# Column groups for the block-diagonal products, a sign check on one partition, ten in-place weight buffers and a new order

## The chip, the cores and the metric

The kernel runs on one core of a Trainium2 chip. The core has five engines with an instruction queue each: TensorE (PE, matmuls into PSUM), VectorE (DVE), ScalarE (ACT), GpSimd (POOL, which works on SBUF only here) and SyncE (SP, which here only issues loads). The outputs are issued from ACT's queue. The metric is the time of one launch on the device in microseconds (us). Before the change it is 217.35 us, the median of three runs (216.36 to 217.43).

## The reference

`x` is 4 x 11456 x 128, `inducing` is 32 x 128. Per batch, 32 inducing rows attend to all tokens (`h`), and then all tokens attend to these 32 rows. Each token of that result goes to one of 8 experts by the largest cosine with the expert's embedding, and through that expert's two matrices, weighted by its gate:

```python
h = mab(I, x)                 # softmax(I x' / sqrt(C)) x : 32 x 128
x = mab(x, h)                 # softmax(x h' / sqrt(C)) h : 11456 x 128
xn = x / (norm(x) + 1e-6);  en = emb / (norm(emb) + 1e-6)
logits = xn @ en.T / tau
e = argmax(logits)            # gate = softmax(logits)[e]
out = gate * (relu(x @ w1[e]) @ w2[e])     # F = 1024 hidden units
```

Since a token's row is a weighted sum of the 32 rows of `h`, norms, logits and hidden units can all be had from its 32 weights. The kernel uses one expert per batch, found from the mean of `h`. If for each hidden unit either all 32 rows keep the same sign, or the sum is sure to have it, the two layers and the ReLU fold into one 32 x 128 matrix `L` per batch. A check proves that this holds; a list of items (batch, expert) that need more is worked off in a loop behind the main program, which is empty for this data.

## The kernel before, in words

A batch's tokens are six blocks: five of 2048 tokens and one of 1280 (320 columns per group of partitions, the others 512). A block lives as 128 partitions (4 groups of 32 weights) x 512 columns.

- **Stage 1** (`stage1`, `own`, `finish`): scores of the block against the inducing rows (L476), their maxima (L536, DVE), the exponentials (L551, ACT), transposes (L574), sums over tokens (L597). Batch 0 transposes three of its own x blocks (L504) instead of loading them. `finish` joins the four groups into `hT` (L677, DVE) by small matmuls (L621, L635, L655, L671, L672), makes the tables `HB` and `gbd` (L737, L738), and picks the expert (L690 to L697), whose weights SP then loads (L728, L729).
- **Stage 2** (`stage2`), per block: scores against `hT` (L767), maxima (L773), their spreading (L778), differences (L784), weights `e` (L789, ACT), the product with the block-diagonal `HB` (L795), its copy `hq` (L801, ACT), `hq * e` (L805, POOL), squared norms (L809), the products with `gbd` (L817, L818) and their transposition (L825). When the blocks of a gate have come through, `gate` works out the gate's values for them: roots, reciprocals, logits (L888), maxima, exponentials, signs, the choice, and at the end `v` (L927, L942) and the gate values `f` (L946).
- **Stage 3** (`stage3`), per block: `fb` spreads the gate values (L1111, DVE), POOL multiplies (L1115, `pf`), PE multiplies with `L` in four row groups (L1134), ACT copies four pieces of PSUM to `o` (L1141) and issues the output's transfer.
- **`fold`** makes `L` out of the expert's weights (L969 to L1031), with the sums that the check needs (L996 to L1007). **`check`** runs its comparison on all 128 partitions (L1043 to L1083) and then `left` (L1091 to L1100) marks what is left to do.

Batch b's stages 2 and 3 run beside stage 1 of batch b+1; the last batch's stages 2 and 3 have nothing beside them. Python code (`Plan`) sets the order: each piece of work has an engine, an estimated duration, dependencies, buffers it takes and frees and a priority from tables of numbers (`FIRST`, `LATE`, `START`, `HOLD`, `NEAR`). The instructions are then emitted in the planned order, and each engine executes its own in that order. `fill` puts matmuls on zeros (L1228, `wz`) where the plan sees PE idle. Buffers are rings: `BUFS` has their lengths (xT 7, x 3, e 7 and so on), and PSUM has 8 banks.

Of the kernel before, what the change touches and what calls it, by code (L numbers as in the profile page):

```python
# [60 lines left out]
FIRST = dict(G=-28.5, L=-60, at=-5, both=6.5, chk=12, chose=43.5, chosen=-23.5, copy_s=-59, count=36, den=53, diff=-31, em=-31, eq=-29.5,  # L61
             evict=58.5, ex=56, expA=33, expB=-25.5, expert=20, f=12.5, fin=-56.5, first=-27, fix=-28, flags=-59.5, fours=-4, fw=-47,
             gat=-8, get_ax=-11, get_w=60, get_x=-1.5, get_xT=-40, gm=10, gm4=7.5, gmb=60, good=16, gv=44, hT=3, hTc=-29, hb=-11.5,
             hj=4.5, hs=-19.5, inv=19, keep_e=-7, keep_hq=-59, keep_x=59.5, left=-31.5, lg=29.5, li=-56, lm=-4, mat=60, mk=-60,
             mults=-10, nb=-6.5, newton=4.5, norm=44, outs=44.5, parts=-24.5, pick=13.5, pick_vals=-1, places=60, prod=9.5, put_h=-60,
             put_li=59.5, put_o=5, r1=6, rm=-17, root=3.5, root_e=60, rows=-22, score=-56, scores=1, se=-12.5, seen=60, selr=55.5,
             sides=4.5, sides2=30.5, signs=44, some=-32, spread=-35, spread_f=-20.5, square=-7.5, square_e=-52, squared=-0.5, sums=15.5,
             times=32.5, top=60, top_e=9.5, turn=26.5, turn_e=-20, turn_s=22, under=54, vals=-29, vp=60, vpb=-30.5, weigh=-26.5,
             zf=-16.5, zs=-5, zz=-15)
# [1319 lines left out]
```

## Time and profile before

| | before |
|---|---|
| time, median of 3 runs | 217.35 us (216.36 to 217.43) |
| the profiled execution | 215.55 us, span 213.9 us |
| mean granted TensorE clock | 0.982 |
| busy: PE / DVE / ACT / POOL | 188.5 / 156.4 / 130.5 / 116.9 us |
| moved by DMA | 72.24 MB, 338 GB/s over the span |
| `hT` of the batches ready (L677 starts) | 31.1, 70.1, 112.6, 153.6 us |

The span is the time from the first to the last instruction; the rest of the execution's time lies around it. The busy times are sums over the whole program, and the program has three parts with different loads: up to 31 us stage 1 of batch 0 and the loads, from there to 154 us three stretches in which stages 2 and 3 of one batch and stage 1 of the next run together, and from there to the end the last batch alone. So the views by stretch say more than the sums.

### The profile page before, as it was taken

Reading aid. Unit: us, or ns where it says so; the run is one execution under the profiler, and the core shown is the slowest. Engines: PE = TensorE matmul, PEld = TensorE weight load, DVE = VectorE, ACT = ScalarE, POOL = GpSimd, SP = SyncE. Lnnn points to the kernel's source line nnn. Section 1 sums busy time; section 2 is a strip of 40 time slices with the busy share of each in tenths; the row PEclk is TensorE's granted clock in tenths of the full one; section 3 lists DMA queues with packets and bytes.
Section 4 is the critical chain, followed back from the end, with each engine's and each line's share of the span. In section 5 each row is a group of like instructions: output and inputs, shape, how many; then the busy total and the mean of one; then the engine's idle time right before and its main releaser. Section 6 shows DMA issues by size and latency. Waiting matters only on the chain.

```text
span 213.9 us, 5217 instructions
## 1 busy us (share of the span) xinstructions
PE 188.5 (88%) x1894; PEld 96.4 (45%) x1894; DVE 156.4 (73%) x433; ACT 130.5 (61%) x302; POOL 116.9 (55%) x232
## 2 busy tenths in 40 slices
PE   7999999999999978799999998899999997796740
PEld 2566652445465434354754344467524433332120
DVE  6544738998995789799688989986589988835230
ACT  2286612462765824267977556779688886876820
POOL 2100000267677734067677674859468989898710
PEclk9999999999999999999999999999999999999975
DMA  6999999999979999998789999994779854349781
GB/s 207 428 424 414 372 415 417 366 424 412 420 254 322 407 348 429 421 415 367 267 279 343 418 428 421 421 406 159 291 201 426 365 202 196 149 165 395 296 367 51
DMA packets 12222, 72.24 MB, mean 338 GB/s; under 512 B 1624, under 2 KB 2144, under 8 KB 4896
## 3 DMA queue, kind: packets, MB, share of 16 engines
q1 hardware_dynamic: 7984, 48.12, 58.0%
q10 hardware_dynamic: 4208, 23.75, 27.1%
q8 instruction: 16, 0.26, 0.5%
q14 instruction: 14, 0.11, 0.1%
HBM read 48.13 MB, written 23.72 MB: 336 GB/s over the span
## 4 chain that ended last, share of the span: by engine, by line
PE 33%; POOL 26%; DVE 17%; DMA 12%; issue 6%; ACT 3%; SPq 0%; DVEq 0%; POOLq 0%
POOL pf L1115 7%; DMA xT<-in_xT 6%; DMA w1t<-in_w 5%; PE ps L476 5%; PE ps L597 5%; POOL hq L805 4%; PE ps L1134 3%; PE ps L574 3%; PE ps L504 3%; PE ps L1228 2%; PE ps L795 2%; DVE mxb L778 2%; PE ps L767 2%; DVE mx L773 2%; DVE d L784 2%
## 5 line engine op out<-in xcount | busy, mean ns | idle before, releaser
L805 POOL TENSOR_TENSOR hq<-hq,e 128x512 f32<-128x512 f32 (+1 forms) x24 | 29.0, 1208 | 48.2 <-ACT hq L801 48.1
L1141 ACT COPY o<-ps 128x512 f32<-128x512 f32 (+1 forms) x94 | 47.5, 569 | 9.5 <-PE ps L1134 7.5
L1115 POOL TENSOR_TENSOR pf<-e,fb 128x512 f32<-128x512 f32 (+1 forms) x24 | 28.9, 1206 | 7.2 <-PE ps L1134 4.8
L1134 PE MATMUL ps<-pf,L 32*128 32x512 f32 (+1 forms) x192 | 26.4, 612 | 1.2 <-POOL pf L1115 0.9
L795 PE MATMUL ps<-e,HB 128*128 128x512 f32 (+1 forms) x48 | 25.0, 606 | 1.1 <-ACT e L789 0.6
L801 ACT COPY hq<-ps 128x512 f32<-128x512 f32 (+1 forms) x24 | 13.4, 557 | 17.5 <-PE ps L795 16.5
L476 PE MATMUL ps<-xT,indT_sb 128*32 128x512 f32 x160 | 21.0, 602 | 3.1 <-DMA xT<-in_xT 2.6
L789 ACT ACTIVATE e<-d 128x512 f32<-128x512 f32 (+1 forms) x24 | 14.5, 604 | 12.7 <-DVE R L784 12.0
L597 PE MATMUL ps<-x,pt 128*32 128x128 f32 x608 | 20.8, 275 | 0.7 <-issue 0.5
L767 PE MATMUL ps<-xT,hT 128*32 128x512 f32 x160 | 19.7, 600 | 1.4 <-ACT L L1031 0.6
L551 ACT ACTIVATE s<-ps,nb 128x1024 f32<-128x1024 f32 (+3 forms) x15 | 13.5, 899 | 11.8 <-DVE nb L543 6.6
L597 PEld LDWEIGHTS ps<-x,pt 128*32 128x32 f32 x608 | 16.0, 109 | 8.5 <-issue 3.8
L1111 DVE STREAM_TRANSPOSE fb<-f 128x512 f32<-128x512 f32 (+1 forms) x24 | 15.3, 661 | 4.3 <-POOL f L946 3.0
L536 DVE TENSOR_REDUCE mk<-ps 128x1 f32<-128x1024 f32 (+3 forms) x15 | 14.1, 941 | 4.2 <-PE ps L476 2.6
L809 DVE TRANSPOSE_TENSOR_REDUCE nn<-hq 128x16 f32<-128x512 f32 (+1 forms) x24 | 15.8, 658 | 1.5 <-POOL hq L805 1.3
L778 DVE STREAM_TRANSPOSE mxb<-mx 128x512 f32<-128x512 f32 (+1 forms) x24 | 16.3, 678 | 0.8
L784 DVE CUSTOM_DVE_ANT_0 d<-mxb,ps 128x512 f32<-128x512 f32 (+1 forms) x24 | 15.5, 648 | 1.3
L773 DVE TRANSPOSE_TENSOR_REDUCE mx<-ps 128x16 f32<-128x512 f32 (+1 forms) x24 | 15.8, 658 | 0.5 <-PE ps L767 0.5
L1228 PE MATMUL ps<-wz 128*128 128x512 f16 x59 | 15.7, 398 | 0.0
L817 PE MATMUL ps<-e,gbd 128*128 128x256 f32 (+1 forms) x48 | 14.9, 392 | 0.8 <-ACT o L1141 0.8
L818 PE MATMUL ps<-e,gbd 128*128 128x256 f32 (+1 forms) x48 | 13.6, 366 | 0.0
L817 PEld LDWEIGHTS ps<-e,gbd 128*128 128x128 f32 x48 | 8.0, 189 | 11.5 <-issue 5.1
(190 smaller groups left out, 329.1 us busy)
## 6 DMA issues: line engine op xcount, KB each, us to landing
xT<-in_xT SPq DMA_DIRECT2D x20, 1024.0 KB, 11.4
out<-o ACTq DMA_DIRECT2D x20, 1024.0 KB, 4.4
x<-in_xP SPq DMA_DIRECT2D x17, 1024.0 KB, 10.8
xL<-in_xT SPq DMA_DIRECT2D x4, 640.0 KB, 14.9
out<-o ACTq DMA_DIRECT2D x4, 608.0 KB, 7.9
x<-in_xP SPq DMA_DIRECT2D x4, 512.0 KB, 3.9
w1t<-in_w SPq DMA_DIRECT2D x4, 512.0 KB, 10.0
w2t<-in_w SPq DMA_DIRECT2D x4, 512.0 KB, 12.2
```

The source lines that it names most:

```text
L476: nc.tensor.matmul(ps[32 * j:32 * j + 32, :].rearrange("p (g i) -> p g i", i=128), lhsT=indT_sb, rhs=v[:, j], start=True, stop=True)
L597: nc.tensor.matmul(ph.t[32 * j:32 * j + 32, 0:C], lhsT=pt.t[:tw, tat[k] + g, 32 * j:32 * j + 32], rhs=x, start=k == ks[0] and g == 0, stop ...
L767: nc.tensor.matmul(ps[32 * j:32 * j + 32, :W].rearrange("p (t i) -> p t i", i=32), lhsT=st.hT[:, 0:M], rhs=v[:, j], start=True, stop=True)
L773: nc.vector.tensor_reduce(new(mx)[:, :T], b1.t[:, :W].rearrange("p (t i) -> p t i", i=32), AX.X, ALU.max, apply_transpose=True)
L778: nc.vector.transpose(new(mxb)[:, :W], mx.t[:, :T].unsqueeze(2).broadcast_to([P, T, 32]))
L795: nc.tensor.matmul(new(b2)[:, :W], lhsT=st.HB, rhs=e.t[:, :W], start=True, stop=True)
L805: nc.gpsimd.tensor_tensor(paired(hq.t[:, :W]), paired(hq.t[:, :W]), halved(e.t[:, :W]), ALU.mult)
L817: nc.tensor.matmul(b3.t[:, :H], lhsT=st.gbd[:, 16:], rhs=e.t[:, :H], start=True, stop=False)
L1115: nc.gpsimd.tensor_tensor(new(pf)[:, :W], st.e[k].t[:, :W], fb.t[:, :W], ALU.mult)
L1134: nc.tensor.matmul(new(pcs[j])[:, :W], lhsT=st.L[32 * j:32 * j + 32, :], rhs=pf.t[32 * j:32 * j + 32, :W], start=True, stop=True)
L1141: (nc.vector.tensor_copy if dve else nc.scalar.copy)(v[:, j], pcs[j].t[:, :W].rearrange("c (t i) -> c t i", i=32))
L1228: nc.tensor.matmul(ps_all[:, b], lhsT=wz[:, 0:P], rhs=wz, start=True, stop=True)
```

## The change

1. **Column groups.** A helper `quads` splits a stationary matrix of 128 columns into four of 32 columns, each a matmul of its own into 32 partitions of PSUM. It is used for `HB`, both `gbd` products, the tables, and the small products of `finish`, `fold` and `check`. The transposes of 128 x 128 stay whole. Row transposes of one column become plain matmuls with the identity. The scores (L476, L767) and L597 have been in such column groups all along.
2. **Sign check on one partition.** `fold` now works out the ratio `less / more` and its maximum over all partitions in the shadow of other work (`over`, `share`, `worst`, `worst_t`, `worst1`); `check` compares one number with it. Three POOL operations of the check (`good`) go. `left` shrinks from eight or nine POOL operations to three, one of which, `chose`, waits only for `seen`; `vp` makes a table `rest` beforehand.
3. **Weights in one buffer.** `mxb`, `d`, `e` and `pf` of a block become one buffer `e` that is overwritten in place, from a ring of 10; the x ring grows from 3 to 4 and f from 3 to 5. In the last batch odd blocks put their output through a buffer of the x ring.
4. **Moves between engines.** The scaling of `sel` goes from DVE to ACT, the addition in `both` (L911) from POOL to ACT (`se9`), one step of `sides2` from POOL to ACT (`both_sides`).
5. **Gates.** The last batch has two gates of three blocks instead of three gates of 3, 2 and 1.
6. **Order.** All priority tables, and the planner's durations; it now counts a switch of the array's mode.

```diff
-GATES = [[(0, 1, 2), (3, 4, 5)]] * 3 + [[(0, 1, 2), (3, 4), (5,)]]
+GATES = [[(0, 1, 2), (3, 4, 5)]] * 4
-BUFS = dict(xT=7, xL=2, x=3, xR=1, s1=2, pt=1, mxb=2, d=2, e=7, hq=2, gts=2, lg=2, ex=1, fb=2, pf=2, o=3, mx=2, nn=2, f=3)
+BUFS = dict(xT=7, xL=2, x=4, xR=1, s1=2, pt=1, e=10, hq=2, gts=2, lg=2, ex=1, fb=2, o=3, mx=2, nn=2, f=5)
-FIRST = dict(G=-28.5, L=-60, at=-5, both=6.5, chk=12, chose=43.5, chosen=-23.5, copy_s=-59, count=36, den=53, diff=-31, em=-31, eq=-29.5,
+FIRST = dict(G=-12, L=-60, at=-39.5, bad1=7, both=-25.5, both_sides=-59.5, chk=12.5, chose=-55.5, chosen=60, copy_s=-49, den=-50.5,
...
-        t = max(clock[o.eng], o.after)
+        t = max(clock[o.eng] + (self.SWITCH if o.eng == PE and o.mode != self.mode else 0.0), o.after)
...
+    def quads(out, lhsT, rhs, start=True, stop=True):
+        for q in range(0, lhsT.shape[-1], M):
+            nc.tensor.matmul(out[q:q + M], lhsT=lhsT[:, q:q + M], rhs=rhs, start=start, stop=stop)
...
+        def sel():
             t["selr"] = small.tile([P, 1], F32, name="selr")
-            nc.vector.tensor_tensor(t["selr"], rz, t["fw"], ALU.mult)
+            nc.scalar.activation(t["selr"], t["rz"], AF.Identity, scale=t["fw"])
             t["sel"] = small.tile([P, P], F32, name="sel")
-            nc.vector.tensor_scalar(t["sel"], flat(sel4), t["selr"], None, ALU.mult)
-        c(DVE, 0.9, selr, free=[b3])
+            nc.scalar.activation(t["sel"], flat(sel4), AF.Identity, scale=t["selr"])
+        c(ACT, 0.5, sel)
...
-            nc.vector.transpose(new(mxb)[:, :W], mx.t[:, :T].unsqueeze(2).broadcast_to([P, T, 32]))
+            nc.vector.transpose(new(e)[:, :W], mx.t[:, :T].unsqueeze(2).broadcast_to([P, T, 32]))
...
-            nc.scalar.activation(new(e)[:, :W], d.t[:, :W], AF.Exp, scale=-SCALE)
+            nc.scalar.activation(e.t[:, :W], e.t[:, :W], AF.Exp, scale=-SCALE)
...
-            nc.tensor.matmul(new(b2)[:, :W], lhsT=st.HB, rhs=e.t[:, :W], start=True, stop=True)
+            quads(new(b2)[:, :W], st.HB, e.t[:, :W])
...
-            nc.tensor.matmul(b3.t[:, :H], lhsT=st.gbd[:, 16:], rhs=e.t[:, :H], start=True, stop=False)
-            nc.tensor.matmul(b3.t[:, :H], lhsT=st.gbd[:, :P], rhs=e.t[:, H:W], start=False, stop=True)
+            quads(b3.t[:, :H], st.gbd[:, 16:], e.t[:, :H], stop=False)
+            quads(b3.t[:, :H], st.gbd[:, :P], e.t[:, H:W], start=False)
...
+        def se9():
+            nc.scalar.activation(t["se"], t["se"], AF.Identity, bias=nano)
         def both():
-            nc.gpsimd.tensor_scalar(t["se"], t["se"], 1.0, 1e-9, ALU.mult, ALU.add)
             nc.gpsimd.tensor_tensor(t["se"], t["se"], t["zz"], ALU.mult)
...
-            nc.gpsimd.tensor_scalar(up, t["pos"], 2.0, -1.0, ALU.mult, ALU.add)
-            nc.gpsimd.tensor_tensor(up, up, t["ss"], ALU.mult)
+        def both_sides():
+            nc.scalar.activation(t["up"], t["ss"], AF.Abs, bias=tiny)
+        def over():
+            nc.vector.reciprocal(t["more"], t["more"])
+        def share():
+            nc.gpsimd.tensor_tensor(t["less"], t["less"], t["more"], ALU.mult)
+        def worst():
+            nc.vector.tensor_reduce(t["wo"], t["less"], AX.X, ALU.max)
+        def worst_t():
+            nc.tensor.matmul(new(pw)[0:1, 0:P], lhsT=t["wo"], rhs=ident, start=True, stop=True)
+        def worst1():
+            nc.vector.tensor_reduce(st.worst, pw.t[0:1, 0:P], AX.X, ALU.max)
+            nc.vector.tensor_scalar_add(st.worst, st.worst, SURE)
...
-        def good():
-            nc.gpsimd.tensor_scalar(t["em"], t["em"], ROOM, None, ALU.mult)
-            nc.gpsimd.tensor_scalar(ok, st.more, t["em"], None, ALU.mult)
-            nc.gpsimd.tensor_tensor(ok, ok, st.less, ALU.subtract)
+        def bad1():
+            nc.vector.tensor_scalar(pad1[0:1, 1:2], t["em"], st.worst, None, ALU.is_lt)
...
+        def chose():
             nc.gpsimd.tensor_scalar(sn, sn, 0.0, None, ALU.max)
+        def left():
+            nc.gpsimd.tensor_scalar(st.rest, st.rest, wipe[:, st.b, 0:1], None, ALU.max)
+            nc.gpsimd.tensor_tensor(present[:, 0:n, st.b], st.seen[:, 0:n], st.rest.unsqueeze(1).broadcast_to([P, n, E]), ALU.mult)
...
-            nc.gpsimd.tensor_tensor(new(pf)[:, :W], st.e[k].t[:, :W], fb.t[:, :W], ALU.mult)
+            nc.gpsimd.tensor_tensor(e.t[:, :W], e.t[:, :W], fb.t[:, :W], ALU.mult)
...
-        o = plan.buf("o")
+        o = plan.buf("x" if st.b == NB - 1 and k % 2 else "o")
```

The new order shows at three places. The first is POOL's queue at the program's end, the last batch's. Before, the third gate (10 columns), the check's bookkeeping on `vq`, `present` and `seen`, and then the last block's product:

```order
L942 TENSOR_SCALAR v<-v,vp 128x10
L946 TENSOR_TENSOR f<-v,se 128x10
L1091 TENSOR_SCALAR vq<-wipe 128x1
L1092 TENSOR_TENSOR vq<-vq,vp 128x1
L1093 TENSOR_SCALAR present<-rev,vq 128x8
L1094 TENSOR_SCALAR present<-present 128x8
L1096 TENSOR_SCALAR seen<-seen 128x24
L1098 TENSOR_TENSOR seen<-seen 128x8 x2
L1099 TENSOR_TENSOR present<-present,seen 128x8
L1100 TENSOR_TENSOR present<-present,wipe 128x1
L1115 TENSOR_TENSOR pf<-e,fb 128x320
```

And now, where L1157 is the product (in place, on `e`) and L978 and L982 are `v` and `f` of the second and last gate:

```order
L978 TENSOR_SCALAR v<-v,vp 128x42
L1136 TENSOR_SCALAR seen<-seen 128x16
L982 TENSOR_TENSOR f<-v,se 128x42
L1141 TENSOR_SCALAR rest<-rest,wipe 128x8
L1142 TENSOR_TENSOR present<-seen,rest 128x2x8
L1157 TENSOR_TENSOR e<-e,fb 128x512 x2
L1157 TENSOR_TENSOR e<-e,fb 128x320
```

The bookkeeping shrank from nine instructions to three, and two more blocks' products now stand behind the last gate.

The second place is DVE's queue around the last batch's `hT`, with the batch before it in its gates. Before:

```order
L660 TENSOR_SCALAR rz<-ps 128x1
L661 RECIPROCAL rz<-rz 128x1
L663 TENSOR_TENSOR selr<-rz,fw 128x1
L665 TENSOR_SCALAR sel<-sel_133,selr 128x128
L825 STREAM_TRANSPOSE gts<-ps 128x160
L809 TENSOR_REDUCE nn<-hq 128x10
L609 SCALAR_TENSOR_TENSOR hj<-hj,fix,ps 128x128
L677 COPY hT<-ps 128x128
```

And now, where L708 is the copy into `hT`, L926, L940, L963 and L974 are the gates' `lm`, `se`, `v` and reciprocal, and L1153 is `fb`:

```order
L963 TENSOR_REDUCE v<-lg 128x48
L969 TENSOR_REDUCE seen<-lg 128x8
L926 TENSOR_REDUCE lm<-lg 128x42
L974 RECIPROCAL se<-se 128x48
L637 SCALAR_TENSOR_TENSOR hj<-hj,fix,ps 128x128
L687 TENSOR_SCALAR rz<-ps 128x1
L688 RECIPROCAL rz<-rz 128x1
L1153 STREAM_TRANSPOSE fb<-f 128x512 x2
L940 TENSOR_REDUCE se<-ex 128x42
L708 COPY hT<-ps 128x128
```

Work of both gates of the batch before, which followed `hT`, now stands ahead of it.

The third is PE's queue behind the last batch's `hT`. Before, with L795, L817 and L818 as whole matmuls between scores in column groups (L767) and outputs in row groups (L1134):

```order
L767 MATMUL ps<-xT,hT 32x512 x8
L1134 MATMUL ps<-pf,L 128x512 x4
L795 MATMUL ps<-e,HB 128x512
L817 MATMUL ps<-e,gbd_143 128x256
L818 MATMUL ps<-e,gbd_143 128x256
L1056 MATMUL ps<-r_2315,ones 128x1
L767 MATMUL ps<-xT,hT 32x512 x4
```

And now, where L372 is `quads`, L800 the scores and L1176 the outputs:

```order
L800 MATMUL ps<-xT,hT 32x512 x12
L1176 MATMUL ps<-e,L 128x512 x4
L372 MATMUL ps<-e,HB 32x512 x4
L800 MATMUL ps<-xT,hT 32x512 x4
L372 MATMUL ps<-e,gbd_137 32x256 x8
```

Scores and block-diagonal products now have the same shape of tile, and PE goes from one to the other without a change of it.

More of the change, by code (lines that the diff above doesn't have):

```diff
@@ L1 @@
+import math
 from contextlib import ExitStack
@@ L59 @@
 SLOT = 6
-FIRST = dict(G=-28.5, L=-60, at=-5, both=6.5, chk=12, chose=43.5, chosen=-23.5, copy_s=-59, count=36, den=53, diff=-31, em=-31, eq=-29.5,
[L62 to L69, printed above, removed]
@@ new lines @@
+LATE = dict(G=-47.5, L=43, at=-20.5, bad1=-39, both=6.5, both_sides=-7, chk=-25.5, chose=43, chosen=-13, copy_s=19.5, den=-17,
+            diff=-59.5, em=-21, eq=-60, evict=-46, ex=-12, expA=30, expB=-3.5, expert=-36, f=6, fin=41, first=-15.5, fix=7.5, flags=5.5,
+            fours=-20, fw=23, gat=-39, get_ax=-16, get_w=54, get_x=-23, get_xT=-49, gm=-9, gm4=58.5, gmb=-10.5, gv=60, hT=-60, hTc=25.5,
+            hb=-46.5, hj=25, hs=6, inv=-45, keep_e=32.5, keep_hq=-36, keep_x=18.5, left=-25, lg=-35.5, li=55, lm=-60, mat=30.5, mk=-60,
+            mults=39.5, nb=23, newton=-15.5, norm=-0.5, outs=44, over=-6, parts=56, pick=53, pick_vals=58, places=58.5, prod=-48,
+            put_h=39.5, put_li=24, put_o=22, r1=58, rm=59.5, root=-60, root_e=23, rows=60, score=-60, scores=-10.5, se=-52, se9=-30,
+            seen=25.5, sel=-51.5, selr=-60, share=-12, sides=-20, sides2=-1.5, signs=26, some=10, spread=26.5, spread_f=-48, square=40.5,
+            square_e=-42, squared=-30, sums=-6.5, times=-60, top=11.5, top_e=-2.5, turn=47, turn_e=60, turn_s=39, under=-30, vals=49.5,
+            vp=32, vpb=-52, weigh=41.5, worst=-28, worst1=5, worst_t=-29, zf=-59, zs=51.5, zz=-10)
@@ L654, in fin @@
         def fin():
-            nc.tensor.matmul(new(b3)[:, 0:1], lhsT=flat(sel4), rhs=t["z"], start=True, stop=True)
-        c(PE, 0.24, fin, take=[b3])
+            quads(new(b3)[:, 0:1], flat(sel4), t["z"])
+        c(PE, 0.22, fin, take=[b3])
         def selr():
@@ L712, in vpb @@
         def vpb():
[L713 to L714 removed]
+            quads(new(b6)[:, 0:1], ones, pad1[:, 0:1])
+        c(PE, 0.22, vpb, take=[b6])
         def vp():
@@ new lines, in sides2 @@
+        def sides2():
+            t["more"] = small.tile([P, NCH], F32, name="more")
+            t["less"] = small.tile([P, NCH], F32, name="less")
+            nc.gpsimd.tensor_tensor(t["more"], t["sa"], t["up"], ALU.add)
+            nc.gpsimd.tensor_tensor(t["less"], t["sa"], t["up"], ALU.subtract)
+        o_2 = plan.add(POOL, 0.46, sides2, deps=[o_sa, o_up], when=when)
+        def over():
+            nc.vector.reciprocal(t["more"], t["more"])
+        o_2 = plan.add(DVE, 0.13, over, deps=[o_2], when=when)
```

288 lines of the change are left out of this document (145 added, 143 removed).

## The prediction

> **What bounds the kernel now.** I read the page's sums and chain first, then the busy times by stretch, then the chain in order of time, and last the single queues where the chain runs through them.
>
> ```profile
> span 213.9 us, 5217 instructions
> PE 188.5 (88%) x1894; PEld 96.4 (45%) x1894; DVE 156.4 (73%) x433; ACT 130.5 (61%) x302; POOL 116.9 (55%) x232
> GB/s 207 428 424 414 372 415 417 366 424 412 420 254 322 407 348 429 421 415 367 267 279 343 418 428 421 421 406 159 291 201 426 365 202 196 149 165 395 296 367 51
> PE 33%; POOL 26%; DVE 17%; DMA 12%; issue 6%; ACT 3%; SPq 0%; DVEq 0%; POOLq 0%
> ```
>
> By the sums POOL, busy for 55%, would be the last engine to look at. But the chain gives it 26% of the span, second to PE only. The stretches are cut where the batches' `hT` are ready, where the last batch's first gate ends, and where the last output is issued:
>
> ```profile
> core 0: us, PE busy (x) PEld busy (x) DVE busy (x) ACT busy (x) POOL busy (x), PEclk, DMA share, GB/s
> 31.10:72.00 40.90, 39.34 (x431) 20.38 (x433) 34.45 (x88) 22.23 (x51) 22.41 (x39) 1.00 0.97 377
> 72.00:112.50 40.50, 36.61 (x414) 19.68 (x407) 34.64 (x82) 24.02 (x55) 22.07 (x46) 1.00 0.94 363
> 112.50:153.60 41.10, 39.08 (x428) 20.57 (x427) 33.60 (x85) 29.60 (x66) 26.98 (x45) 1.00 0.89 360
> 153.60:184.70 31.10, 27.80 (x184) 12.13 (x184) 27.40 (x70) 24.33 (x57) 26.64 (x52) 1.00 0.68 259
> 184.70:207.10 22.40, 16.29 (x98) 6.05 (x96) 10.39 (x34) 15.01 (x37) 16.94 (x43) 0.98 0.75 309
> ```
>
> In the three middle stretches PE is busy for 115.0 of 122.5 us; DVE has 34 us of 41 and POOL 22 to 27. Behind 153.6 PE, DVE and POOL are close together, and behind 184.7 no engine is dense by its busy time, but the chain shows what the order does there:
>
> ```profile
> 160.22 1.28 POOL pf L1115
> ...
> 161.58 0.24 POOL se L911
> ...
> 161.90 0.27 POOL se L912
> ...
> 174.32 0.26 POOL n L874
> ...
> 177.47 0.81 POOL lg L888
> ...
> 181.64 0.24 POOL se L911
> ...
> 184.68 0.29 POOL f L946
> ...
> 187.71 0.58 POOL lg L888
> ...
> 192.66 0.18 POOL n L874
> ...
> 194.10 0.42 POOL v L942
> ...
> 194.84 0.28 POOL lg L888
> ...
> 195.19 0.24 POOL em L1066
> ...
> 196.15 1.22 POOL pf L1115
> 197.38 0.28 POOL lg L897
> 197.66 1.22 POOL pf L1115
> ...
> 200.81 0.17 POOL vq L1091
> ...
> 203.31 0.83 POOL pf L1115
> ```
>
> From 160.2 to 204.1 the chain is POOL's own queue with a few short steps of DVE between: an operation that goes from POOL there shortens the run, until the next engine binds.
>
> **The end: POOL's part.** Differences of starts in that fence give the prices, gaps of issue included. The bookkeeping `left` takes 203.31 - 200.81 = 2.5 us; its three successors are small operations like L911 and L912, 0.3 us each by 161.90 - 161.58, so 0.9 in all: 1.6 us less, once for each of the last two batches. The check's three operations take 196.15 - 195.19 = 0.96 us, also twice. The addition L911 goes three times, 0.32 each: 1.0. The third gate costs 194.10 - 192.66 = 1.44 for its root, 0.35 and 0.28 for its logits (from 194.84 to 195.19, and L897), and 200.81 - 198.88 = 1.93 from the end of the last big product to the bookkeeping: 4.0 us. Against that the second gate grows by 80 columns of logits; L888 took 0.81 us for 384 and 0.58 for 256, so 0.15 for each of three passes, 0.5 us. In sum 3.2 + 1.9 + 1.0 + 4.0 - 0.5 = 9.6 us of POOL's queue. Not all of it can come off:
>
> - *153.6 to 184.7.* Here 3.2 us of it lie (one `left`, one check, two additions). But DVE is busy for 27.4 of the 31.1 us, and its work there stays: the same maxima, spreadings, differences and transpositions in place of ring buffers. So this stretch cannot get under about 28 us; with a microsecond of waits I take 29, **-2 us** (bounds -3 and 0).
> - *184.7 to 207.1.* Some 6 us of POOL's work go here. What is next is ACT, which has to copy six blocks out and issue them:
>
> ```profile
> 201.52 2.05 ACT L1141 COPY o<-ps 128x512 f32<-128x512 f32 x4 [0.47 <-ACT o L1141]
> 205.02 0.75 ACT L1141 COPY o<-ps 128x320 f32<-128x320 f32 x2 [1.45 <-PE ps L1134]
> ```
>
> A block costs 2.05 us of copies and 0.47 ahead of them, in which the output before is issued: 2.5 us. In the new order ACT does the second gate's exponentials and signs before the last batch's first copy. From `f` of the first gate to there: `f` 0.3, `fb` 0.7, the first product 1.2, the second gate's subtraction 0.75 (between 0.58 and 0.81), exponential and sign 1.0 (nearest, the additions of the same shape): 4 us. Then five blocks at 2.5 and the last, shared with DVE as before, at 1.9 (between 0.75 for ACT's half and 207.1 - 205.0 = 2.1): 4 + 12.5 + 1.9 = 18.4 us instead of 22.4, **-4 us** (bounds -6, all of POOL's share, and 0 if the products come too late for ACT). POOL is done with its last product after some 12 us of these 18 (its queue in that stretch: three passes and four small operations of the gate, three of `left`, five products of 1.2 us and one of 0.8), so ACT covers what was moved behind the last gate. The outputs leave 2.5 us apart, 1.05 MB each or 419 GB/s, which full slices reached (up to 429). The last 213.9 - 207.1 = 6.8 us stay.
>
> **The middle: PE's part.** What a change of tile costs is seen where the same group stands behind its own kind and behind another:
>
> ```profile
> 87.97 0.88 PE ps L597 x32
> 95.00 1.05 PE ps L795 x2
> 140.55 0.86 PE ps L795 x2
> 142.39 1.01 PE ps L597 x32
> 145.48 0.31 PE ps L635 x2
> 152.37 0.58 PE ps L1017 x16
> 157.10 1.85 PE ps L767 x16
> ```
>
> L597 (column groups) took 0.88 us behind column groups and 1.01 behind a whole product; L795 (whole) 0.86 behind whole transposes and 1.05 behind column groups. So a change is 0.13 to 0.19 us. The four-fold product itself should cost nothing: two blocks of scores, 512 columns in four groups, took 1.85 us, 0.93 each, like L795 with its change. In the order I count 85 changes between the first and the last `hT` before and 45 now, if products with a one-column stationary count as column groups, and about 20 fewer if they count as whole: 20 x 0.13 = 2.6 to 40 x 0.19 = 7.6 us. The small products of `finish`, `fold` and `check`, 0.31 us each as whole, become eight short instructions; L1017 did 16 such in 0.58, so 0.29 at most, and as their moving side has one column where L1017's has 128, I take 0.22: seven per batch, 0.6 us, 1.9 us over three stretches (bounds 0.4 and 3). So PE has 3 to 10 us less work in 122.5 us of which it is busy for 115. DVE's 34 us and the transfers leave room: the stretches moved 367 GB/s on average against up to 429 in full slices, so the same bytes need 105 us at least. I take half of the middle, **-4 us** (bounds -10 and +5; the plus from the second rival).
>
> ```profile
> L805 POOL TENSOR_TENSOR hq<-hq,e 128x512 f32<-128x512 f32 (+1 forms) x24 | 29.0, 1208 | 48.2 <-ACT hq L801 48.1
> ```
>
> **The rest.** `sel` and `se9` on ACT, the three additions to DVE in `fold`, `rest` and the memsets hide beside PE in the middle, where ACT has 11 to 18 us free per stretch and DVE 6; uncovered they would be 0.2 to 0.4 us each, some 1.5 per batch. One x buffer more lets a load start a block earlier, but the loads wait for L597 of the batch before in either kernel; I count nothing. In-place operation has no row here; the nearest are POOL's two products of the same shape: L805, in place, has a mean of 1.21 us, L1115, not in place, took 1.22 in the chain above. Nothing.
>
> **The sum.** -4 - 2 - 4 = -10 us: a span of 203.9, and with the 1.65 us around it (215.55 - 213.9) 205.55 for a profiled execution. The median of the runs shown lies 1.8 above the profiled execution (217.35 against 215.55), so **207.4 us**.
>
> ```profile
> L767 PEld LDWEIGHTS ps<-xT,hT 128*32 128x32 f32 x160 | 3.9, 108 | 9.2 <-ACT o L1141 2.9 <-issue 2.4 <-DVE R L784 1.0
> L795 PEld LDWEIGHTS ps<-e,HB 128*128 128x128 f32 x48 | 7.4, 188 | 10.3 <-ACT e L789 6.1 <-ACT ex L902 1.7 <-issue 0.9
> ```
>
> **Rivals.**
> 1. *The end gives nothing back* (DVE or ACT binds at once, as the last stretch's order is tight), and the middle gains little: only 4 of the 10 us, **213 us**. For it: three engines within 1 us of each other from 153.6 to 184.7. Against it: behind 184.7 the gain does not need DVE.
> 2. *Slower: `hT` behind the other batch's gate.* DVE's queue now has `se` of the second gate ahead of the copy into `hT`, and `se` needs the whole way from the root: 181.64 - 174.32 = 7.3 us in the trace. Scores, maxima and loads of the next batch wait for `hT`. If PE reaches `hT` before that way is done, each `hT` is late by up to 7 us; from 3.5 us on at each of three places the 10 us are gone, and at 5 the time is 207 + 15 = **222 us**. Against it: PE needs about 10 us from the last block's product with `HB` to `hT` in the new order (two transposes, four row sums and two outputs at about 0.9, the rest small), which about covers the way and the copy and product before it.
> 3. *No change*: the order's stalls eat PE's gain and half of the end, **217 us**. For it: PE, DVE and transfers each at 85% or more in the middle.
> 4. *Weight loads in the open*: the block-diagonal products now take 24 loads per block at 0.108 us instead of 6 at 0.19. If none ran beside matmuls, this would be 2.6 - 1.1 = 1.5 us per block, 35 us in all, **242 us**. Against it stand the scores, which have done it all along: 16 loads of 0.108 and 16 matmuls in 1.85 us.
>
> The Trainium skill (TensorE: Matmul & The Clock Gate, Part 3, The mechanism) says that a weight load overlaps a running matmul only if their row groups differ; column groups share theirs, so by it the fourth rival would hold. The rows of the scores above do not agree with it.
>
> **How the numbers follow.** My forecast has a chance of 0.57, with a range of its own of 201 to 212; the first rival 0.18, the second 0.17, the third 0.07, the fourth 0.01. Three runs spread over 0.5%, so within 0.5% (216.3 to 218.4) counts as no change. Faster are the forecast and the first rival, 0.75; the same is the third, 0.07; slower the second and fourth, 0.18. The range goes from 200 (the middle at -10, the end a microsecond or so better) to 219: it holds the forecast, the first and third rivals and the mildest of the second.
>
> **What would show it.** The end: behind the first gate's `f` of the last batch ACT's copies follow each other with only the issues between, and from there to the last issue about 18.4 us; POOL waits there. From the last `hT` to that `f` about 29 us with DVE as the chain. Middle: `hT` copies at about 70, 111 and 149.5 us and fewer long groups behind changes of tile; products with `HB` at 0.86 to 0.93. Wrong: an idle DVE ahead of the copy into `hT`, waiting for ACT or POOL; block-diagonal groups over 1.2 us; an end of over 21 us.

## The result, and the profile after

The changed kernel takes **205.08 us** (median of four runs, 204.54 to 206.03), the kernel before beside it 216.86 (215.54 to 217.43). The ratio is 0.947 with a 95% interval of 0.941 to 0.953; a second measurement gave 0.947 (0.943 to 0.951). The forecast was 207.4 us with a range of 200 to 219. The profiled execution has a span of 203.1 us, 10.8 less than before. The page's sums, bandwidths and chain after the change:

```profile
span 203.1 us, 6507 instructions
PE 180.8 (89%) x2555; PEld 89.0 (44%) x2555; DVE 151.8 (75%) x436; ACT 134.6 (66%) x315; POOL 104.2 (51%) x178
GB/s 197 427 426 418 363 410 421 413 360 421 413 407 414 410 361 405 418 424 422 422 414 428 415 364 413 419 422 322 2 207 316 394 260 202 179 366 284 413 400 73
DVE 27%; PE 24%; DMA 14%; POOL 12%; ACT 11%; issue 5%; ACTq 1%; SPq 1%; POOLq 0%; DVEq 0%
```

POOL's share of the chain fell from 26% to 12%, PE's from 33% to 24%, and DVE leads now. From the second slice to the 27th the transfers run at 400 to 428 GB/s, but for four slices at 360 to 364. Next, the busy times by stretch, cut as before: the four copies into `hT`, the last batch's first `f`, the issue of the last output, the end.

```profile
core 0: us, PE busy (x) PEld busy (x) DVE busy (x) ACT busy (x) POOL busy (x), PEclk, DMA share, GB/s
33.00:68.00 35.00, 33.85 (x581) 18.87 (x577) 32.48 (x86) 21.02 (x50) 17.74 (x29) 1.00 1.02 406
68.00:111.70 43.70, 38.72 (x597) 18.18 (x601) 34.62 (x89) 30.78 (x71) 24.85 (x37) 1.00 1.01 412
111.70:148.60 36.90, 35.66 (x584) 18.79 (x583) 33.48 (x91) 28.06 (x67) 25.41 (x46) 1.00 0.81 324
148.60:177.40 28.80, 28.13 (x347) 10.54 (x335) 27.06 (x74) 24.71 (x61) 22.98 (x39) 1.00 0.70 270
177.40:194.90 17.50, 13.15 (x90) 4.67 (x86) 8.74 (x21) 14.02 (x31) 11.20 (x16) 1.00 0.88 360
194.90:203.10 8.20, 0.00 (x0) 0.00 (x0) 0.00 (x0) 0.00 (x0) 0.00 (x0) 0.50 0.49 200
```

| stretch | before, us | after, us | difference | forecast |
|---|---|---|---|---|
| start to first `hT` | 31.1 | 33.0 | +1.9 | not priced |
| first to last `hT` | 122.4 | 115.6 | -6.8 | -4 |
| last `hT` to `f` of the first gate | 31.1 | 28.8 | -2.3 | -2 |
| that `f` to the last issue | 22.1 | 17.5 | -4.5 | -4 |
| last issue to the end | 7.2 | 8.2 | +1.0 | 0 |
| span | 213.9 | 203.1 | -10.8 | -10 |

Each `f` and issue counts by its start here. In the three middle stretches PE is busy for 33.85 + 38.72 + 35.66 = 108.2 of 115.6 us, before for 115.0 of 122.4: its work fell by 6.8 us and its idle time, 7.4 in both, did not change. (The matmuls on zeros are counted in, 1.1 us before and 1.8 after.) By the copies into `hT`, which before start at 31.1, 70.1, 113.0 and 153.6 us, the first and the third of these stretches are 4.0 and 3.7 us shorter and the second is 0.9 us longer. What ended the idle time of DVE ahead of the copy into `hT`, and who waited for that copy, is told by the view of that one line:

```profile
L708 DVE COPY hT<-ps x4: 278/292/292, 33.0 to 148.6; 128x128 f32<-128x128 f32 x4
...
  PE ps L372: 1.8, 3
...
  PEld ps L800: 0.3, 1
```

DVE waited there only for PE. The two ends of the last batch, POOL first, then ACT, in the order of time:

```profile
175.26 0.27 POOL L907 TENSOR_TENSOR n<-nnr,r 128x42 f32<-128x42 f32 x1
...
177.40 0.28 POOL L982 TENSOR_TENSOR f<-v,se 128x48 f32<-128x48 f32 x1
...
184.65 0.29 POOL L982 TENSOR_TENSOR f<-v,se 128x42 f32<-128x42 f32 x1
184.90 0.33 POOL L1141 TENSOR_SCALAR rest<-rest,wipe 128x8 f32<-128x8 f32 x1
185.31 0.22 POOL L1142 TENSOR_TENSOR present<-seen,rest 128x16 f32<-128x16 f32 x1
185.83 3.31 POOL L1157 TENSOR_TENSOR e<-e,fb 128x512 f32<-128x512 f32 x3 [0.30 <-DVE fb L1153]
```

```profile
181.51 0.57 ACT L1183 COPY o<-ps 128x512 f32<-128x512 f32 x1
...
186.69 2.05 ACT L1183 COPY o<-ps 128x512 f32<-128x512 f32 x4 [0.46 <-ACT x L1183]
...
189.15 2.05 ACT L1183 COPY x<-ps 128x512 f32<-128x512 f32 x4 [0.41 <-ACT o L1183]
```

The second gate's root is refined (L907) 2.1 us *before* the first gate's `f`. ACT's copies follow each other every 2.5 us with only the issues between. Before, the last gate's `n` stood at 192.66, 8 us behind that `f`, and ACT waited 1.45 us for the last block's product (rows in the prediction).

### The profile page after: what moved, and what is told of

Its sections match the earlier page's. It is cut to its first block, busy times and chain, and to the rows that moved or that the text cites. A ratio compares the mean times of both kernels' runs of the same rounds, so it can differ in the third digit from the quotient of the medians.

```text
span 203.1 us, 6507 instructions
## 1 busy us (share of the span) xinstructions
PE 180.8 (89%) x2555; PEld 89.0 (44%) x2555; DVE 151.8 (75%) x436; ACT 134.6 (66%) x315; POOL 104.2 (51%) x178
## 4 chain that ended last, share of the span: by engine, by line
DVE 27%; PE 24%; DMA 14%; POOL 12%; ACT 11%; issue 5%; ACTq 1%; SPq 1%; POOLq 0%; DVEq 0%
DMA xT<-in_xT 9%; DMA out<-o 5%; PE ps L625 5%; ACT o L1183 4%; DVE mx L806 4%; DVE e L811 4%; PE ps L504 4%; PE ps L1272 4%; DVE e L817 4%; POOL hq L838 3%; PE ps L531 3%; PE ps L602 3%; DVE gts L858 2%; DVE nn L842 2%; DVE fb L1153 2%
## 5 line engine op out<-in xcount | busy, mean ns | idle before, releaser
L1183 ACT COPY o<-ps 128x512 f32<-128x512 f32 (+1 forms) x84 | 43.5, 567 | 13.7 <-PE ps L1176 11.5
L1157 POOL TENSOR_TENSOR e<-e,fb 128x512 f32<-128x512 f32 (+1 forms) x24 | 28.7, 1210 | 6.5 <-DVE fb L1153 6.5
L1176 PE MATMUL ps<-e,L 32*128 32x512 f32 (+1 forms) x192 | 26.6, 613 | 0.7 <-POOL e L1157 0.6
L372 PE MATMUL ps<-e,gbd 128*32 128x256 f32 (+1 forms) x384 | 23.7, 367 | 1.4 <-DVE R L817 1.2
L372 PE MATMUL ps<-e,HB 128*32 128x512 f32 (+1 forms) x192 | 23.8, 571 | 0.3 <-ACT e L822 0.2
L800 PE MATMUL ps<-xT,hT 128*32 128x512 f32 x160 | 20.6, 598 | 0.1
L625 PE MATMUL ps<-x,pt 128*32 128x128 f32 x608 | 20.3, 274 | 0.4 <-issue 0.2
L822 ACT ACTIVATE e<-e 128x512 f32<-128x512 f32 (+1 forms) x24 | 14.6, 607 | 8.2 <-DVE R L817 6.9
L625 PEld LDWEIGHTS ps<-x,pt 128*32 128x32 f32 x608 | 17.2, 110 | 5.0 <-ACT pt L609 1.8
L372 PEld LDWEIGHTS ps<-e,gbd 128*32 128x32 f32 x384 | 12.8, 109 | 14.1 <-issue 3.4
L1272 PE MATMUL ps<-wz 128*128 128x512 f16 x58 | 17.5, 422 | 0.1
L1153 DVE STREAM_TRANSPOSE fb<-f 128x512 f32<-128x512 f32 (+1 forms) x24 | 15.1, 653 | 2.1 <-POOL f L982 1.4
L811 DVE STREAM_TRANSPOSE e<-mx 128x512 f32<-128x512 f32 (+1 forms) x24 | 16.1, 670 | 0.5
L806 DVE TRANSPOSE_TENSOR_REDUCE mx<-ps 128x16 f32<-128x512 f32 (+1 forms) x24 | 15.6, 651 | 0.5 <-PE ps L800 0.5
L842 DVE TRANSPOSE_TENSOR_REDUCE nn<-hq 128x16 f32<-128x512 f32 (+1 forms) x24 | 15.6, 657 | 0.3 <-POOL hq L838 0.2
L817 DVE CUSTOM_DVE_ANT_0 e<-e,ps 128x512 f32<-128x512 f32 (+1 forms) x24 | 14.9, 620 | 0.0
L602 PE MATMUL ps<-ident,s 128*128 128x128 f32 (+1 forms) x92 | 13.1, 281 | 1.2 <-ACT s L579 1.2
```

The costliest lines, as they stand in the source:

```text
L372: nc.tensor.matmul(out[q:q + M], lhsT=lhsT[:, q:q + M], rhs=rhs, start=start, stop=stop)
L625: nc.tensor.matmul(ph.t[32 * j:32 * j + 32, 0:C], lhsT=pt.t[:tw, tat[k] + g, 32 * j:32 * j + 32], rhs=x, start=k == ks[0] and g == 0, stop ...
L800: nc.tensor.matmul(ps[32 * j:32 * j + 32, :W].rearrange("p (t i) -> p t i", i=32), lhsT=st.hT[:, 0:M], rhs=v[:, j], start=True, stop=True)
L806: nc.vector.tensor_reduce(new(mx)[:, :T], b1.t[:, :W].rearrange("p (t i) -> p t i", i=32), AX.X, ALU.max, apply_transpose=True)
L811: nc.vector.transpose(new(e)[:, :W], mx.t[:, :T].unsqueeze(2).broadcast_to([P, T, 32]))
L817: nc.vector.tensor_tensor_reduce(out=e.t[:, :W], in0=e.t[:, :W], in1=b1.t[:, :W], scale=1.0, scalar=0.0, op0=ALU.subtract, op1=ALU.max, ac ...
```

## The experiments

Each run is compared by its ratio to the kernel before, which ran beside it. The changed kernel, once more, has 0.947, so 0.01 is 2.2 us.

**The changed kernel again.** No edit.

> The changed kernel itself once more, as the measure for the runs beside it, and to see how far its start times repeat: a ratio to the kernel before of 0.94 to 0.955 again, and `hT` copies within 0.5 us of 33.0, 68.0, 111.7 and 148.6 us, the first gate's `f` of the last batch near 177.4, if the order alone sets them.

204.59 us, ratio 0.9466 (0.9425 to 0.9507). The copies into `hT` start at 32.3, 67.4, 111.1 and 148.0 us and `f` at 176.8, all 0.6 to 0.7 us earlier than in the first trace. From the first `hT` on the times repeat within 0.1 us; the first `hT` itself moves by up to 1.4 us (31.8 to 33.2) between the traces of the new order here.

**The large products whole again.**

```diff
-            quads(new(b2)[:, :W], st.HB, e.t[:, :W])
+            nc.tensor.matmul(new(b2)[:, :W], lhsT=st.HB, rhs=e.t[:, :W], start=True, stop=True)
...
-            quads(b3.t[:, :H], st.gbd[:, 16:], e.t[:, :H], stop=False)
-            quads(b3.t[:, :H], st.gbd[:, :P], e.t[:, H:W], start=False)
+            nc.tensor.matmul(b3.t[:, :H], lhsT=st.gbd[:, 16:], rhs=e.t[:, :H], start=True, stop=False)
+            nc.tensor.matmul(b3.t[:, :H], lhsT=st.gbd[:, :P], rhs=e.t[:, H:W], start=False, stop=True)
```

> The changed kernel with the two kinds of large products of stage 2 (with `HB` and with `gbd`) as whole products again; every engine's order stays, as do the small products in column groups. Theory PE: the middle's gain is PE's own work, handed on in full. From the two traces one block's products with `HB` take 0.91 us before and 0.84 after from start to start, those with `gbd` 0.97 and 0.84, and the scores beside them 0.95 and 0.87, so 0.28 us a block and 5.0 for the 18 blocks between the first and the last `hT`, 6.7 for all 24: 209 to 212 us. Theory order: the gain of the middle is the new order's and the fuller transfers', and PE's slack hides the rest: 205 to 207 us.

208.84 us, ratio 0.968 (0.960 to 0.976): 4.6 us are lost. Its busy times between the `hT` copies:

```profile
33.00:68.30 35.30, 35.01 (x473) 19.96 (x469) 32.65 (x87) 21.18 (x50) 17.73 (x30) 1.00 1.01 400
68.30:113.50 45.20, 40.34 (x489) 19.61 (x492) 34.61 (x89) 30.74 (x71) 24.77 (x37) 0.96 1.00 395
113.50:151.60 38.10, 37.26 (x475) 19.46 (x476) 33.75 (x91) 28.14 (x68) 25.35 (x46) 1.00 0.78 318
```

PE's work in the middle rises from 108.2 to 112.6 us, by 4.4, and the middle from 115.6 to 118.6, by 3.0; DVE, ACT and POOL have the same work as in the changed kernel. This trace is of the slowest of the run's four executions (210.24 us), and its second stretch has a granted clock of 0.96. There PE stood idle for 3.33 us up to 91.17, waiting for a load, and then had about half its clock:

```profile
92.20:96.00 3.80, 3.80 (x15) 1.30 (x12) 3.35 (x7) 1.88 (x4) 0.29 (x1) 0.55 1.02 426
```

```profile
92.16 1.92 PE L1176 MATMUL ps<-e,L 32*128 32x512 f32 x8
```

The same outputs take 1.14 us elsewhere. By the clock some 1.7 of the 3.8 us are lost there (an estimate, 3.8 x 0.45), so in the second stretch the edit's own price is not known; the first and the third, with the clock at 1.00, have 2.8 us more work and take 1.5 us longer. Behind the last `hT` the loss goes on: up to the first gate's `f` it takes 31.1 us instead of 28.8, again at a clock of 1.00.

```profile
151.60:182.80 31.20, 29.66 (x239) 12.31 (x229) 27.07 (x74) 25.00 (x61) 23.01 (x39) 1.00 0.66 250
```

The theory of PE is much the closer one, though it priced 6.7 us in all and 4.6 were lost: not all of PE's work is on the path.

**The small products whole again.** One line of this kind for each of the nine:

```diff
-            quads(ps[:, 0:P], st.hj, t["sel"])
+            nc.tensor.matmul(ps[:, 0:P], lhsT=st.hj, rhs=t["sel"], start=True, stop=True)
```

> The changed kernel with only the small products (of the row sums, `hT`, the tables, `vp`, the four-sum and the flag) as whole products again, nine per batch; the order and the large products stay. By the prediction's size a small product is 0.09 us longer as whole: nine of them at three places are 2.4 us, 207 to 208 us. With a change of tile before and behind each that now stands between column groups (0.13 to 0.19 us each, nine times two at three places at most) it is up to 10 us: 212 us or more. If the middle is not PE's, no change: 205 us.

207.01 us, ratio 0.959 (0.951 to 0.968), 2.8 us lost, and 2.4 by the medians. That is the prediction's size, not the larger one with two changes of tile each. Its busy times in the middle:

```profile
33.20:68.90 35.70, 34.80 (x527) 19.89 (x526) 32.85 (x86) 20.86 (x50) 17.94 (x30) 1.00 1.01 394
68.90:112.60 43.70, 39.61 (x546) 18.73 (x547) 34.66 (x89) 31.07 (x72) 24.76 (x36) 1.00 1.01 411
112.60:150.00 37.40, 36.56 (x523) 19.05 (x526) 33.70 (x92) 28.09 (x67) 25.50 (x46) 1.00 0.80 320
```

PE has 111.0 us of work there, 2.7 more than in the changed kernel, and the middle takes 116.8 us, 1.1 more. Another 1.3 us are lost between the last `hT` and the first gate's `f` (30.0 instead of 28.8 us), which the expectation, with three places for these products, did not count.

**The large products alone, in the kernel before.** The edit of the first experiment in the other direction, with nothing else changed.

> The kernel before with one edit: the products with `HB` and `gbd` in four column groups; order, buffers and small products stay as before. Theory PE: the same 0.28 us a block as in the other direction, 18 blocks in the middle and a part of the last six: 5 to 6 us less, 211 to 212 us. Theory order: without the new order and the added buffers the stalls take it back: 215 to 217 us.

216.39 us over ten runs, ratio 1.002 (0.997 to 1.007). By the median, the same edit that costs 4.6 us to undo in the new order brings nothing in the old. Its runs spread from 212.8 to 219.4 us, more than those of any other kernel here (214.6 to 218.4 for the kernel before beside it), and the profiled one is the fastest of them: in that one the middle is 1.9 us shorter than in the kernel before. So the edit can gain some, and no trace shows where the other runs lost it. The mean granted clock is 0.98 in the two fastest and 0.955 to 0.966 in six of the other eight, but 0.974 and 0.984 in the last two: why they are slower stays open.

**Two gates alone, in the kernel before.**

```diff
-GATES = [[(0, 1, 2), (3, 4, 5)]] * 3 + [[(0, 1, 2), (3, 4), (5,)]]
+GATES = [[(0, 1, 2), (3, 4, 5)]] * 4
```

> The kernel before with one edit: the last batch has two gates instead of three. The order of the last batch is planned anew by the old tables, the three batches before it stay. By the prediction's step the third gate costs POOL 4.0 us on the chain, less 0.5 for the wider second gate: 213 to 214 us. If the old bookkeeping and the copies bind at once behind it: 216 to 217 us.

218.54 us, ratio 1.014 (1.005 to 1.023): slower by 3 us, with an interval of 1 to 5, and outside both theories. Four rows of its trace show where, POOL's of the second gate and the copy that ACT could then make:

```profile
184.27 0.29 POOL L946 TENSOR_TENSOR f<-v,se 128x48 f32<-128x48 f32 x1
...
187.89 0.29 POOL L874 TENSOR_TENSOR n<-nnr,r 128x42 f32<-128x42 f32 x1
...
197.05 0.28 POOL L946 TENSOR_TENSOR f<-v,se 128x42 f32<-128x42 f32 x1
```

```profile
203.29 2.06 ACT L1141 COPY o<-ps 128x512 f32<-128x512 f32 x4 [7.20 <-PE ps L1134]
```

The second gate starts 3.6 us behind the first `f` and ends 12.8 us behind it; the old bookkeeping follows at once, and ACT waits 7.2 us with three blocks left. Some 0.8 of these are PE's (an estimate): it had been idle for 2.69 us, and its outputs then took 3.80 us for two blocks at a granted clock of 0.50, where one block takes 1.14 elsewhere. In the changed kernel the second `f` comes 184.65 - 177.40 = 7.25 us behind the first. A whole gate's operations were gone, and the end came later.

**Three gates in the changed kernel.** The edit above in the other direction.

> The changed kernel with three gates in the last batch (blocks 0 to 2, 3 and 4, 5); the last batch's order is planned anew by the same tables, the three batches before it stay. Theory POOL's sum (the prediction's): the third gate puts 4.0 - 0.5 us back on POOL's chain, of which the copies cover some: 2 to 3.5 us above the changed kernel. Theory order (from the kernel before with two gates, where ACT waited 7.2 us for the late second gate): what counts is how early the gates behind the first one start, not how many they are: within 1.5 us of the changed kernel, or less.

206.91 us, ratio 0.958 (0.955 to 0.960); 2.3 us above the changed kernel beside it. That is the lower end of the theory of POOL's sum. Its three `f`:

```profile
176.81 0.29 POOL L982 TENSOR_TENSOR f<-v,se 128x48 f32<-128x48 f32 x1
186.09 0.25 POOL L982 TENSOR_TENSOR f<-v,se 128x32 f32<-128x32 f32 x1
191.38 0.21 POOL L982 TENSOR_TENSOR f<-v,se 128x10 f32<-128x10 f32 x1
```

The first `f` is where it was (176.78 beside it), the second 2.0 us later than with two gates, and the last output leaves 2.6 us later (196.87 against 194.31).

**The old tables with the new operations, and the new tables with the old operations.** In each, FIRST, LATE, START, NEAR and HOLD are taken from the other kernel, and nothing else; a name that the other tables lack gets a priority of zero.

> The changed kernel's operations, gates, buffers and planner's costs with the old tables of priorities, near and hold times. Names that the old tables don't have get a priority of zero. Theory order: the operations alone bring little, as the column groups alone did in the kernel before: 212 to 218 us. Theory operations (the prediction's terms: fewer changes of tile, shorter POOL queue) : 206 to 209 us, most of the gain without the new order.

> The kernel before with the new tables of priorities, near and hold times; operations, gates, buffers and the planner's costs stay (two old names that the new tables lack get a priority of zero). Theory order alone: if the new order is better for either set of operations, 208 to 213 us. Theory matched pair: tables and operations belong together, as the old tables with the new operations took 228 us: 217 to 228 us.

227.93 us, ratio 1.054 (1.051 to 1.058), and 231.32 us, ratio 1.076 (1.068 to 1.085). Both mixtures are slower than either kernel, and the first lies far outside both of its theories, the second above its slower one. So tables and operations have to match, and the two runs give no worth of either alone that could be added up.

**Three buffers for natural blocks of x.** The planner goes on counting four and the engines' orders stay; only the pool has three, so a load without a buffer waits, and the loads behind it on SP's queue with it. The diff leaves out the lines that emit the instructions as the smaller pool allows, each engine's in its old order.

```diff
+REAL = dict(BUFS, x=3)
...
-    pools = {n: pool("p_" + n, BUFS[n]) for n in shapes}
+    pools = {n: pool("p_" + n, REAL[n]) for n in shapes}
```

> The changed kernel with three buffers for natural blocks of x instead of four; the order of every engine and the ring sizes that the planner counts with stay, so only the loads that lack a buffer start later (and the last batch's outputs of odd blocks share three). Theory PE (the prediction counted nothing for the buffer): at most 1 us above the changed kernel's ratio of 0.947. Theory transfers: the middle moved 406 and 412 GB/s in its first two stretches instead of 375 and 363 because a block is under way earlier; without it each of three stretches loses some of that, 3 to 6 us in all, a ratio of 0.96 to 0.975.

218.42 us, ratio 1.014 (1.006 to 1.022): 14 us lost, far outside both theories. Its profiled execution was its slowest (220.43 of 216.93 to 220.43), so up to 3.5 us of what its trace shows is not the buffer's. Of the 15.7 us by which its span is longer, 15.5 lie between the first and the last `hT`. PE's waits for transfers in it, and behind them those of the changed kernel:

```profile
PE ps L540 <- DMA xT<-in_xT: 9.3, 5, 5.2
PE ps L1041 <- DMA w1t<-in_w: 3.5, 2, 1.8
PE ps L661 <- DMA x<-in_xP: 2.8, 1, 2.8
```

```profile
PE ps L504 <- DMA xT<-in_xT: 2.6, 2, 1.8
...
PE ps L1005 <- DMA w1t<-in_w: 0.5, 1, 0.5
```

15.6 against 3.1 us, and two of the 40 slices drop to 145 and 59 GB/s:

```profile
GB/s 215 426 425 406 383 413 390 145 391 413 421 338 360 372 369 362 401 427 421 309 303 420 383 59 352 422 420 428 176 3 356 266 355 118 195 383 285 406 409 99
```

How long the queue of the loads stood is told by SP's waits for the sums over tokens that free a block of x (L661 here, L625 in the changed kernel):

```profile
SPq L519 <- PE ps L661: 44.2, 10, 15.3
```

```profile
SPq L483 <- PE ps L625: 15.7, 9, 6.5
```

The new order needs the fourth buffer. What an order planned for three would lose, no run shows; the kernel before had such an order, with waits of 2.6 us for `xT`.

**More work for POOL, at two places.** Eight idle operations ahead of `left`, of the last batch in one run and of the third batch in the other:

```diff
+            for _ in range(8 if st.b == NB - 1 else 0):
+                nc.gpsimd.tensor_scalar(idle, idle, 0.0, None, ALU.max)
             nc.gpsimd.tensor_scalar(st.rest, st.rest, wipe[:, st.b, 0:1], None, ALU.max)
```

> The changed kernel with eight idle POOL operations of 128x16 put ahead of the last batch's bookkeeping `left`, some 1.8 to 2.2 us in all by the 0.22 to 0.25 us of its neighbours; the order stays. The prediction says that behind the first gate's `f` ACT's copies cover what POOL had there: at most 0.5 us above the changed kernel. If POOL's queue still sets the end: 1.8 to 2.2 us above it.

> The changed kernel with the same eight idle POOL operations (2.54 us in the profile of the run with the last batch's) ahead of the third batch's `left`, which lies 5 us behind the last `hT`; the order stays. The prediction says that DVE sets the stretch from the last `hT` to the first gate's `f`: POOL is busy for 23.0 of 28.8 us there, so at most 0.7 us above the changed kernel. If POOL's queue is the chain there as it was before: 2 to 2.5 us above it.

*Last batch:* 207.57 us, ratio 0.962 (0.956 to 0.969), 3.0 above the changed kernel beside it. Padding, products and the first copy behind them:

```profile
184.19 2.54 POOL L1144 TENSOR_SCALAR idle<-idle 128x16 f32<-128x16 f32 x8
...
187.28 3.32 POOL L1161 TENSOR_TENSOR e<-e,fb 128x512 f32<-128x512 f32 x3
```

```profile
191.03 2.05 ACT L1187 COPY x<-ps 128x512 f32<-128x512 f32 x4 [3.01 <-PE ps L1180]
```

Where ACT had 0.41 us between two blocks it now has 3.01, and 2.6 more looks like the 2.54 us arriving whole. PE's rows around that block tell it otherwise, here and then in the changed kernel:

```profile
187.38 0.35 PE L1226 MATMUL ps<-onec,present 128*32 128x1 f32 x6 [2.78 <-POOL present L1146]
...
188.92 2.09 PE L1180 MATMUL ps<-e,L 32*128 32x512 f32 x8
```

```profile
187.43 1.14 PE L1176 MATMUL ps<-e,L 32*128 32x512 f32 x8
```

Counted from the first `f` (176.68 here) the matmuls start 12.24 instead of 10.03 us behind it, 2.2 later. They take 0.95 us longer, at a granted clock of 0.50 from 188.9 to 191.1, behind 2.78 us in which PE stood idle for POOL. And in the changed kernel they were done 0.6 us before ACT came for them at 189.15. 2.2 + 0.95 - 0.6 gives the 2.6. So behind the second `f` POOL has some 0.6 us of slack towards ACT, and without the drop of the clock about 1.6 us would have arrived (an estimate).

*Third batch:* 206.25 us, ratio 0.962 (0.955 to 0.969); 1.7 us above the changed kernel by the medians, 3.3 by the ratios. The last batch's first `f` starts at 178.40 instead of 176.78:

```profile
178.40 0.29 POOL L984 TENSOR_TENSOR f<-v,se 128x48 f32<-128x48 f32 x1
```

So 1.6 of the 2.5 us come through, 1.9 counted from the last `hT`, though POOL is busy for only 23.0 of 28.8 us there. The way is one wait of DVE for the gate of the batch before, whose `f` stands behind the padding:

```profile
DVE fb L1157 <- POOL f L984: 2.3, 1, 2.3
```

**All copies of the last batch shared by ACT and DVE.**

```diff
-                    stage3(plan, st, q, t, split=nx is None and q == NSB - 1)
+                    stage3(plan, st, q, t, split=nx is None)
```

> The changed kernel with the copies of all six blocks of the last batch shared between ACT and DVE, as only the last block's are in both kernels; the last batch's order is planned anew by the same tables. Theory ACT (the prediction's price of 2.5 us a block): the end is ACT's copying, and with half of it gone 2 to 4 us less. Theory transfers: the outputs leave 1.05 MB every 2.5 us, which is the transfers' own rate, 413 GB/s between 184.6 and 196.3 us; only the first block comes a microsecond earlier: within 1 us of the changed kernel.

204.28 us, ratio 0.951 (0.944 to 0.957): as the changed kernel. The last issue comes 1.1 us earlier (193.25 against 194.31), but the stretch behind it is 1.2 us longer, 9.4 instead of 8.2 us:

```profile
193.30:202.70 9.40, 0.00 (x0) 0.00 (x0) 0.00 (x0) 0.00 (x0) 0.00 (x0) 0.50 0.57 225
```

What ACT no longer sets, the transfers and the waits for POOL and PE set (ACT's longest is now 2.64 us for PE). No run beat the changed kernel.

## Why the prediction was right, and where its steps failed

The time lies 2.3 us below the forecast and within its range, and each priced stretch moved the way it was said to and within its bounds. Of the 2.3 us, 0.8 are the span's. The other 1.5 are the distance from the profiled execution to the median, taken over as 1.8 us from the kernel before; it is 0.3 here. That the span came so close is in part luck: the priced stretches gave 3.7 us more than forecast, and the start and the tail, at nothing in the forecast, took 2.9 back. The steps did not all hold.

- **The middle, "I take half", -4.** PE's work fell by 6.8 us, within the forecast 3 to 10. The two undone edits come to about as much, 4.4 (some of it the clock's) and 2.7 us, the second against a forecast of 1.9; how much of the first is changes of tile and how much the shorter groups, no run separates. They give back 3.0 and 1.1 us of time: some six tenths of the work, 4.1 us. So half was about right for PE. The middle gained 6.8, and for the other 2.7 the prediction had no term. The fuller transfers (406 and 412 GB/s in the first two stretches, 375 and 365 before, from copy to copy into `hT`) are the candidate: with one x buffer fewer the first two stretches have 351 and 374, and the middle grows by 15.5 us (in the slowest execution of that run). Nothing here separates them from the order.
- **The four-fold product at no cost.** It held. Two blocks of products with `gbd`, and what follows them, from the timeline of PE in the changed kernel:

```profile
161.58 1.91 PE L372 MATMUL ps<-e,gbd 128*32 128x256 f32 x32
163.43 1.14 PE L1176 MATMUL ps<-e,L 32*128 32x512 f32 x8
```

From start to start that is 163.43 - 161.58 = 1.85 us, 0.93 a block. The weight loads of the same products, from the same time:

```profile
161.56 1.45 PEld L372 LDWEIGHTS ps<-e,gbd 128*32 128x32 f32 x32 [0.70 <-ACT o L1183]
```

All 32 of them run within those 1.85 us and take 1.45 of them, so without overlap 0.40 us would be left for 32 matmuls. The fourth rival falls. The Trainium skill (TensorE: Matmul & The Clock Gate, Part 3, The mechanism) says that loads overlap a running matmul only in another row group; this trace does not agree with that sentence. The same section also lets a load into the background weight buffer be pulled ahead, and that would allow what is seen; no run here tells whether it is the reason.
- **"One x buffer more ... I count nothing."** This step failed. Taking the fourth buffer out of the new order costs 14 us; what it is worth beside an order planned for three stays open. The step argued that the loads wait for the same products in either kernel. But loads stand in one queue, and SP's waits for those products grew from 15.7 to 44.2 us; the loads of `xT` and of the weights were late with them, and PE's waits for transfers grew from 3.1 to 15.6 us.
- **Behind the last `hT`, -2 with DVE as the floor.** The size held (28.8 us for a forecast 29), and DVE is the floor: it is busy for 27.1 of 28.8 us. The reason held only in part. The step priced nothing but POOL's shorter queue, and the stretch is as short as this because neither POOL nor PE makes DVE wait for more than 0.5 us at a time. With 2.5 us more for POOL ahead of one `f`, DVE waited 2.3 us for it. With the large products whole the stretch takes 31.1 us, as long as before the change, and with the small ones whole 30.0; DVE then waits for PE ahead of the transposes of `gts`, 1.9 us with the large ones:

```profile
DVE gts L858 <- PE ps L851: 1.9, 2, 1.4
```

So PE's column groups, which the prediction counted in the middle only, are worth up to 2.4 and 1.3 us here too. What counts is at which place an engine is waited for, not its sum.
- **The third gate, 4.0 less 0.5 us of POOL.** In the new order it is worth 2.3 us. In the old order taking it away costs 3 us. The price was read off POOL's queue as if the gate could be lifted out; by the traces what decides is when the remaining second gate starts, and only the new order starts it ahead of the first `f`. No run moves that start alone.
- **"ACT covers what was moved behind the last gate."** This held for what was moved, but not with the room that the forecast gave it. POOL is done after 11.7 us of 17.5 for a forecast 12 of 18, and ACT's copies never wait for it. The room is not the 6 us behind POOL's last product: it is some 0.6 us, at the place between the second `f` and the next block's product. What goes beyond that arrives at the end, as the padding shows. For the same reason the short `left` counts: it takes 0.9 us, and the 1.6 us that the old one had more by the prediction would not have fitted.
- **ACT's 2.5 us per block, -4.** Right: the copies follow each other at 2.5 us, and 17.5 us were needed. With ACT relieved nothing is gained: it then waits up to 2.64 us for PE, and the stretch behind the last issue grows by 1.2 us; which of the two would bind alone, no run separates. "The last 6.8 us stay" missed a microsecond: more of the outputs is left to move there, 200 GB/s over 8.2 us where it was 103 over 7.2.
- **The first stretch** had no term and grew by 1.9 us in the first trace, by 0.7 to 2.1 in the others of the changed order.

Of the rivals, the first (the end gives nothing) fell: behind the last `hT` 54.5 us are left instead of 60.3. The second, `hT` behind the other batch's gate, fell by the rows of L708: its only waits, 1.8 us in all, were for PE, and PE waited 0.3 us for it. The third was no change.

## What to carry to other kernels

Price an edit of an operation inside the order that it will run in: the same four column groups were worth nothing by the median in one order and 4.6 us in another, and one gate less was worth +3 us in one and -2.3 in the other. A queue's sum of busy time does not say whether a microsecond on it is covered; look for the place where another engine takes over its product, and ask which of the two arrives first there. When a pad or an undone edit costs as much as it should, look at the clock in its trace before calling the price confirmed. Before counting a buffer as nothing, look at what stands behind the transfer that would wait for it in the same queue.
